# A new order for the opening of a Fourier mixing and ELU kernel: x by two queues, weights converted in three steps

## The chip, the core and the metric

The kernel runs on one core of a Trainium2 chip. The metric is the device time of one launch in microseconds (us). The kernel before took 2698.89 us, the median of three runs (2695.69 to 2701.08).

A core has five engines that run side by side and each keep the order of their own instructions: PE (TensorE, matrix products), DVE (VectorE), ACT (ScalarE), POOL (GpSimd) and SP (SyncE, which here only issues transfers). Transfers (DMA) are issued by SP and ACT on one kind of queue and by POOL on another. Engines wait for each other where data or a buffer needs it.

## The reference, cut to what matters

```python
# x (8, 3008, 256), filt_r and filt_i (1505, 256), all float32
X = np.fft.rfft(x, axis=1)
y = np.fft.irfft(X * (filt_r + 1j * filt_i)[None], n=3008, axis=1).astype(np.float32)

h = y.reshape(24064, 256) @ w_in             # w_in (256, 2048)
g = np.where(h > 0, h, np.exp(np.minimum(h, 0.0)) - 1.0)
out = (g @ w_out).astype(np.float32)         # w_out (2048, 256)
```

Both weights arrive as float64, and the kernel computes in float32. It fetches each number as a pair of 32-bit words and builds the float32 from the bits: this is the "conversion" that the text is about.

## The kernel before: what the change touches

The transform of length 3008 is done as 47 x 64 with small matrix products, and goes through memory (DRAM) twice: z holds the sums over 64, yd holds the first half of the way back. For a batch b the units are:

- `x_load`, `x_unit` (DVE: sum and difference), `a_unit` (PE psa, ACT copies), `z_write`: six chunks c.
- `z_read`, `b_unit` (PE psr, psi; DVE four products with the filter f; POOL subtracts and adds), `bi_unit` (PE pva, pvb; ACT copies), `y_write`: eight groups g.
- `y_read`, `n_unit` (PE psn, ACT copies, DVE four sums): six row blocks m.
- Then per block four "quads" q, a quarter of the 2048 columns each: `up_steps` (seven products with w_in[q], PE phs, pha, phd, with copies and ELU on ACT and DVE) and, a quad later, `down_steps` (seven products with w_out[q], PE po).

The first batch's transform stands alone in the opening; those of the other seven lie between quads. In the opening the filters are read into one large buffer ff, whose padding must be zero. In the quads w_in[q] is first needed in quad q, and w_out[q] in quad q + 1.

The 16 pieces of weights (512 KB each) are numbered k; q = k // 4, pieces 0 and 1 of four belong to w_in[q], 2 and 3 to w_out[q]. After the second of each pair four sums (s1, s2, s4, a21) prepare the seven-product scheme. One piece, before:

```python
def w_convert(k):
    wd = wds.pop(k)
    lo, hi = wd[:, :, 0], wd[:, :, 1]
    m, e = (kp.tile([P, 512], U32, tag=t, name=n) for t, n in (("k0", "wm"), ("k1", "we")))
    fl = kp.tile([P, 2, 512], FP32, tag="c", name="wfl")          # kp has one buffer of each
    f, l = fl[:, 0], fl[:, 1]
    nc.vector.tensor_scalar(out=m, in0=hi, scalar1=0x000FFFFF, scalar2=None, op0=ALU.bitwise_and)   # L509
    nc.scalar.activation(out=l, in_=lo, func=AXT.Identity, scale=2.0 ** -52)                        # L510
    nc.scalar.activation(out=f, in_=m, func=AXT.Identity, scale=2.0 ** -20, bias=1.0)               # L511
    nc.vector.tensor_scalar(out=e, in0=hi, scalar1=20, scalar2=0x7FF,
                            op0=ALU.logical_shift_right, op1=ALU.bitwise_and)                       # L513
    nc.vector.tensor_scalar(out=e, in0=e, scalar1=1151.0, scalar2=896.0, op0=ALU.min, op1=ALU.max)  # L515
    nc.vector.tensor_scalar(out=e, in0=e, scalar1=896.0, scalar2=8388608.0,
                            op0=ALU.subtract, op1=ALU.mult)                                         # L516
    nc.vector.scalar_tensor_tensor(out=e, in0=hi, scalar=0x80000000, in1=e,
                                   op0=ALU.bitwise_and, op1=ALU.bitwise_or)                         # L518
    nc.vector.tensor_tensor(out=f, in0=f, in1=l, op=ALU.add)                                        # L520
    # ... dst = f * e, one or two instructions (L528, L531)
    if j % 2 == 1:
        # ... the four sums (L535 to L538)
```

The opening, before:

```python
CONVERTS = {1: 6, 3: 7, 5: 8, 7: 9, 8: 10, 9: 11}
for k in range(2):
    w_fetch(k)                                  # POOL's queue
for c in range(NXC):                            # x: SP's queue, its table: ACT's
    x_load(0, c, nc.scalar, more[c - XBUFS] if c >= XBUFS else None)
nc.gpsimd.memset(ff, 0.0)
# ... gb, gr, gi
wait_x(3)                                       # POOL waits for the fourth chunk of x
w_fetch(2)
w_fetch(3)
wait_x(5)
for a in range(2):
    f_read_first(ff, a)                         # POOL's queue, 24 transfers
for c in range(NXC):
    x_unit(0, c); a_unit(0, c); z_write(0, c)
    if c in (0, 2):
        w_convert(c // 2)
for k in range(4, 7):
    w_fetch(k)
for k in range(2, 6):
    w_convert(k)
    w_fetch(k + 5)
z_read(0, 0); z_read(0, 1)
for g in range(NG + 2):
    if g >= 2: bi_unit(0, g - 2)
    if g < NG:
        b_unit(0, g, ff[:, g])
        if g + 2 < NG: z_read(0, g + 2)
    if g >= 2: y_write(0, g - 2)
    if g in CONVERTS: w_convert(CONVERTS[g])
    # ... w_fetch 11 and 12, x_load(1, 0) and (1, 1)
y_read(0, 0)
w_convert(12)
# ... POOL waits for y, then w_fetch 13, 14, 15
n_unit(0, 0)
# quads: w_convert 13 and 14 at the end of quad 0, 15 at the end of quad 1
```

Of the kernel before, what the change touches and what calls it, by code (L numbers as in the profile page):

```python
# [10 lines left out]
FP32 = mybir.dt.float32  # L11
# [10 lines left out]
N = 3008  # L22
# [78 lines left out]
def kernel(  # L101
# [38 lines left out]
    w_in, w_out = ([glob.tile([P, 7, 2, P], FP32, name="%s%d" % (n, i)) for i in range(4)] for n in ("wi", "wo"))  # L140

    fbufs = [glob.tile([P, 2, 2, D], FP32, name="f%d" % i) for i in range(FBUFS)]
    junk = glob.tile([P, 1], FP32, name="junk")
    fd = fdp.tile([NG, 2, 48, 2, 2, D], FP32, name="fd")

    xs, tas, tns, t1s, t2s, ss, t3s, t4s, zs, yds, ys, g_of, po_of, cs_, sds = ({} for _ in range(15))
# [1 line left out]
    def raw(src, row, ap, col=0):  # L148
        return bass.AP(tensor=src.tensor, offset=src.offset + row * D + col, ap=ap)
# [8 lines left out]

    def x_load(b, c, queue=nc.sync, place=None):

        t, w = place or (xp.tile([P, 2, 2, D], FP32, tag="xc", name="xc"), tap.tile([P, 2, P], FP32, tag="ta", name="ta"))
        xs[b, c], tas[b, c] = t, w
        queue.dma_start(w, ta_d[:, 2 * c:2 * c + 2, :])
        for h in range(2):
            i = XC * c + 2 * h
            r = slice(64 * h, 64 * h + 32)
            nc.sync.dma_start(t[r].rearrange("p k u d -> p k (u d)"),
                              raw(x, b * N + i, [[N1 * D, 32], [32 * N1 * D, 2], [1, 2 * D]]))  # L170
            r = slice(64 * h + 32, 64 * h + 64)
            for u in range(2):
                if i + u == 0:
                    nc.gpsimd.memset(t[r, :, 0, :], 0.0)
                else:
                    nc.sync.dma_start(t[r, :, u, :],  # L176
                                      raw(x, b * N + N1 - i - u, [[N1 * D, 32], [32 * N1 * D, 2], [1, D]]))

    def x_unit(b, c):
        t = xs[b, c]  # L180
# [299 lines left out]
    def w_fetch(k):  # L480
        q, j = divmod(k, 4)

        wd = wds[k] = wbufs[k % 5 if k < 12 else (2, 0, 1, 2)[k - 12]].bitcast(U32).rearrange("p c u d -> p (c u d)").rearrange("p (a w) -> p a w", w=2)
        if j < 2:
            srcs = [moe_w_in.bitcast(U32)[ts(j, P), ts(q, 1024)]]
        else:
            srcs = [moe_w_out.bitcast(U32)[ts(4 * q + 2 * (j - 2) + i, P), :] for i in range(2)]
        for i, s in enumerate(srcs):
            n = 512 // len(srcs)
            nc.gpsimd.dma_start(wd[:, ts(i, n), :].rearrange("p a w -> p (a w)"), s)  # L490

    def w_convert(k):

        q, j = divmod(k, 4)
        if j < 2:
            dst = w_in[q][:, 2 * j:2 * j + 2, :, :].rearrange("p j a c -> p a j c")
            shape = dict(a=2, j=2)
        else:  # L500
            dst = w_out[q][:, 0:4, j - 2, :]
            shape = None
        wd = wds.pop(k)
        lo, hi = wd[:, :, 0], wd[:, :, 1]
        m, e = (kp.tile([P, 512], U32, tag=t, name=n) for t, n in (("k0", "wm"), ("k1", "we")))
        fl = kp.tile([P, 2, 512], FP32, tag="c", name="wfl")
        f, l = fl[:, 0], fl[:, 1]

        nc.vector.tensor_scalar(out=m, in0=hi, scalar1=0x000FFFFF, scalar2=None, op0=ALU.bitwise_and)  # L509
        nc.scalar.activation(out=l, in_=lo, func=AXT.Identity, scale=2.0 ** -52)  # L510
        nc.scalar.activation(out=f, in_=m, func=AXT.Identity, scale=2.0 ** -20, bias=1.0)  # L511

        nc.vector.tensor_scalar(out=e, in0=hi, scalar1=20, scalar2=0x7FF,  # L513
                                op0=ALU.logical_shift_right, op1=ALU.bitwise_and)
        nc.vector.tensor_scalar(out=e, in0=e, scalar1=1151.0, scalar2=896.0, op0=ALU.min, op1=ALU.max)  # L515
        nc.vector.tensor_scalar(out=e, in0=e, scalar1=896.0, scalar2=8388608.0,  # L516
                                op0=ALU.subtract, op1=ALU.mult)
        nc.vector.scalar_tensor_tensor(out=e, in0=hi, scalar=0x80000000, in1=e,  # L518
                                       op0=ALU.bitwise_and, op1=ALU.bitwise_or)
        nc.vector.tensor_tensor(out=f, in0=f, in1=l, op=ALU.add)  # L520
        if shape:
            f, e = (t.rearrange("p (a j c) -> p a j c", **shape) for t in (f, e.bitcast(FP32)))
        else:

            f, e = (t.rearrange("p (i a e s) -> p i e a s", i=2, a=4, e=2) for t in (f, e.bitcast(FP32)))
            dst = dst.rearrange("p (i e) (a s) -> p i e a s", i=2, a=4)
        if shape:
            nc.vector.tensor_tensor(out=dst, in0=f, in1=e, op=ALU.mult)  # L528
        else:
            for i in range(2):  # L530
                nc.vector.tensor_tensor(out=dst[:, i], in0=f[:, i], in1=e[:, i], op=ALU.mult)  # L531
        if j % 2 == 1:
            w = (w_in if j < 2 else w_out)[q]
            a11, a21, a12, a22, s1, s2, s4 = (w[:, i] for i in range(7))
            nc.vector.tensor_tensor(out=s1, in0=a21, in1=a22, op=ALU.add)  # L535
            nc.vector.tensor_tensor(out=s2, in0=s1, in1=a11, op=ALU.subtract)
            nc.vector.tensor_tensor(out=s4, in0=a12, in1=s2, op=ALU.subtract)
            nc.vector.tensor_tensor(out=a21, in0=a11, in1=a21, op=ALU.subtract)  # L538

    def f_arrange():  # L540

# [16 lines left out]
    with tc.manual_schedule():  # L558


        CONVERTS = {1: 6, 3: 7, 5: 8, 7: 9, 8: 10, 9: 11}
        with tc.tile_pool(name="boot", bufs=1) as bp:
            ff = bp.tile([P, NG, 2, 2, D], FP32, name="ff")
            wbufs += [bp.tile([P, 2, 2, D], FP32, name="wb%d" % i) for i in range(2)]
            more = [(bp.tile([P, 2, 2, D], FP32, name="xb%d" % i), bp.tile([P, 2, P], FP32, name="tb%d" % i))
                    for i in range(NXC - XBUFS)]

            def wait_x(c):

                nc.gpsimd.tensor_copy(out=junk[0:1], in_=xs[0, c][0:1, 0, 0, 0:1])  # L570

            for k in range(2):
                w_fetch(k)
            for c in range(NXC):
                x_load(0, c, nc.scalar, more[c - XBUFS] if c >= XBUFS else None)
            nc.gpsimd.memset(ff, 0.0)
            for t, d in ((gb, gb_d), (gr, gr_d), (gi, gi_d)):
                nc.gpsimd.dma_start(t, d)
            wait_x(3)
            w_fetch(2)  # L580
            w_fetch(3)
            wait_x(5)
            for a in range(2):
                f_read_first(ff, a)
            for c in range(NXC):
                x_unit(0, c)
                a_unit(0, c)
                z_write(0, c)
                if c in (0, 2):
                    w_convert(c // 2)  # L590
            for k in range(4, 7):
                w_fetch(k)
            for k in range(2, 6):
                w_convert(k)
                w_fetch(k + 5)
            z_read(0, 0)
            z_read(0, 1)
            for g in range(NG + 2):
                if g >= 2:
                    bi_unit(0, g - 2)  # L600
                if g < NG:
                    b_unit(0, g, ff[:, g])
                    if g + 2 < NG:
                        z_read(0, g + 2)
                if g >= 2:
                    y_write(0, g - 2)
                if g in CONVERTS:
                    w_convert(CONVERTS[g])
                if g == 1:
                    w_fetch(11)  # L610
                if g == 4:
                    w_fetch(12)
                if g in (5, 6):
                    x_load(1, g - 5)
        yp = pool("yp", 2)
        gp = pool("gp", 2)
        ep = pool("ep", 2)
        op = pool("op", 1)
        y_read(0, 0)
        w_convert(12)  # L620
        nc.gpsimd.tensor_copy(out=junk[0:1], in_=t4s[0, 0][0:1, 0, 0:1])
        for k in (13, 14, 15):
            w_fetch(k)
        n_unit(0, 0)

# [3 lines left out]
        def at(quad, place, fn, *a):  # L631
            plan.setdefault((quad, place), []).append((fn, a))

        for c in range(2, XBUFS):
            at(c - 2, 0, x_load, 1, c)
        for k in (13, 14, 15):
            at(max(k - 14, 0), 1, w_convert, k)
        at(3, 1, f_arrange)
        for f in fbufs:
            at(4, 1, nc.vector.memset, f, 0.0)  # L640
        for b in range(B):
            t = (b - 1) * PER
            if b > 0:
                for c, s in enumerate((0, 2, 3, 4, 6, 7)):
                    at(t + s - 1, 0, x_unit, b, c)
                    at(t + s, 0, a_unit, b, c)
                    nb, nxt = (b, c + XBUFS) if c + XBUFS < NXC else (b + 1, c + XBUFS - NXC)
                    if nb < B:
                        at(t + s, 0, x_load, nb, nxt)
                    at(t + s, 0, z_write, b, c)  # L650
# [72 lines left out]
```

## Time and profile before

All from one profiled launch, whose span was 2697.7 us.

| engine | busy us | share of the span |
|---|---|---|
| PE | 2593.4 | 96% |
| DVE | 1870.0 | 69% |
| ACT | 1474.7 | 55% |
| POOL | 279.9 | 10% |

PE is the bound on average. But the page also cuts the span into 40 slices of 67 us and gives the busy share of each in tenths: PE has 1 and 6 in the first two and 9 in nearly all others. The opening is thus a stage of its own and is to be read by itself: in the timeline (instructions in order of time, with the idle time ahead of each and who ended it), in the chain of waits (followed back from the last instruction) and in busy times by stretch. "PEclk" is the clock that PE was granted, as a share of full speed; "DMA" the mean busy share of the 16 transfer engines. Some events of the opening:

| event | us from the start |
|---|---|
| first chunk of x in use (DVE) | 12.48 |
| POOL sees the last chunk of x | 29.06 |
| first z transfer issued | 28.45 |
| first transfer of the filters issued | 29.63 |
| first product with the filter (DVE) | 72.36 |
| last group's products begin | 114.50 |
| first matmul psn | 133.91 |
| PE without gaps from about | 174.60 |

In a line such as `90.02 1.11 DVE L509 TENSOR_SCALAR wm<-f 128x512 ...` the first number is the start, the second the duration, L509 the line of the kernel, and `wm<-f` says that tile wm is written from f.

### The profile page before, as it was taken

How to read it: one execution, taken by the hardware profiler on the slowest of the kernel's cores; microseconds unless marked ns; L12 is line 12 of the kernel's file. 1: busy time of each engine (PE TensorE's matmuls, PEld its weight loads, DVE VectorE, ACT ScalarE, POOL GpSimd, SP SyncE). 2: the span in 40 equal slices, each digit the busy share in tenths (PEclk: the TensorE clock that was granted, in tenths of full speed). 3: DMA queues.
4: the chain of work that ended last, by engine and by line, in shares of the span. 5: the costliest groups of instructions: out<-in, count | busy, mean ns of one | idle time of the engine just before them, and what ended most of it. 6: DMA issues, size and time to landing. Idle time of an engine off the chain costs nothing.

```text
span 2697.7 us, 37154 instructions
## 1 busy us (share of the span) xinstructions
PE 2593.4 (96%) x13376; PEld 2196.4 (81%) x13376; DVE 1870.0 (69%) x3243; ACT 1474.7 (55%) x2561; POOL 279.9 (10%) x325
## 2 busy tenths in 40 slices
PE   1689999999999999999999999999999999999998
PEld 1278888987889878988889887898789888899887
DVE  4876776667667677767766677676767767666665
ACT  2255555555556555555555555565556555555554
POOL 4311210002100120001200021000210012000000
PEclk7589999999999999999999999999999999999999
DMA  9545331434213431153314332143421233110010
GB/s 232 156 121 132 79 78 40 101 77 104 62 38 89 103 96 38 45 124 79 85 37 91 90 90 70 38 101 83 114 58 38 60 87 92 38 40 19 21 27 16
DMA packets 234934, 208.23 MB, mean 77 GB/s; under 512 B 134052, under 2 KB 201142, under 8 KB 234752
## 3 DMA queue, kind: packets, MB, share of 16 engines
q1 hardware_dynamic: 216096, 168.15, 25.3%
q0 software_dynamic: 17792, 36.93, 5.6%
q8 instruction: 106, 1.74, 0.3%
q10 hardware_dynamic: 864, 0.79, 0.1%
q14 instruction: 76, 0.62, 0.1%
HBM read 130.68 MB, written 78.12 MB: 77 GB/s over the span
## 4 chain that ended last, share of the span: by engine, by line
PE 94%; DMA 2%; DVE 2%; issue 1%; SPq 0%; ACT 0%; POOL 0%; ACTq 0%; DVEq 0%; POOLq 0%
PE po L426 42%; PE phs L344 25%; PE phd L344 12%; PE pha L344 6%; PE psn L296 3%; PE pva L239 2%; PE psr L239 2%; PE psa L194 2%; DMA z<-t 0%; DMA ff<-in_filt_i_dram 0%; DMA ta<-ta_t 0%; PE pvb L239 0%; SPq L176 0%; DMA t<-z 0%; DMA xb<-in_x_dram 0%
## 5 line engine op out<-in xcount | busy, mean ns | idle before, releaser
L426 PE MATMUL po<-g,wo 128*128 128x256 f32 (+1 forms) x5376 | 1298.1, 376 | 0.0
L426 PEld LDWEIGHTS po<-g,wo 128*128 128x128 f32 x5376 | 1016.3, 190 | 129.4 <-issue 15.4
L355 ACT ACTIVATE g<-phs 128x512 f32<-128x512 f32 (+1 forms) x576 | 339.0, 589 | 845.3 <-PE phs L344 844.6
L352 DVE TENSOR_TENSOR g<-phd,g 128x512 f32<-128x512 f32 (+1 forms) x384 | 259.6, 676 | 462.8 <-ACT e L362 277.8
L362 ACT ACTIVATE e<-e 128x512 f32<-128x512 f32 (+1 forms) x768 | 477.3, 622 | 24.4
L344 PE MATMUL phs<-ys,wi 128*128 128x256 f32 (+1 forms) x1536 | 388.9, 376 | 11.2 <-ACT g L355 11.2
L344 PE MATMUL phs<-y,wi 128*128 128x256 f32 (+1 forms) x1536 | 395.5, 380 | 0.0
L366 DVE SCALAR_TENSOR_TENSOR g<-e,g 128x512 f32<-128x512 f32 (+1 forms) x576 | 387.2, 672 | 0.0
L361 ACT ACTIVATE e<-g 128x512 f32<-128x512 f32 (+1 forms) x576 | 352.8, 613 | 36.7 <-DVE g L352 30.6
L344 PEld LDWEIGHTS phs<-y,wi 128*128 128x128 f32 x1536 | 285.1, 190 | 82.9 <-ACT t L267 34.1
L344 PEld LDWEIGHTS phs<-ys,wi 128*128 128x128 f32 x1536 | 292.4, 191 | 45.4 <-ACT g L355 12.3
L366 DVE SCALAR_TENSOR_TENSOR g<-e,phs 128x512 f32<-128x512 f32 (+1 forms) x192 | 130.0, 677 | 139.6 <-ACT e L362 139.6
L256 POOL TENSOR_TENSOR sr<-sr,sp 128x512 f32<-128x512 f32 x64 | 81.2, 1269 | 1265.3 <-DVE sp L253 1265.3
L344 PE MATMUL phd<-ys,wi 128*128 128x256 f32 (+1 forms) x768 | 193.9, 375 | 1.8 <-DVE g L352 1.8
L344 PE MATMUL pha<-y,wi 128*128 128x256 f32 (+1 forms) x768 | 194.0, 375 | 0.0
L344 PE MATMUL phd<-y,wi 128*128 128x256 f32 (+1 forms) x768 | 193.9, 375 | 0.0
L361 ACT ACTIVATE e<-phs 128x512 f32<-128x512 f32 (+1 forms) x192 | 113.0, 588 | 140.5 <-PE phs L344 139.6
L344 PEld LDWEIGHTS phd<-ys,wi 128*128 128x128 f32 x768 | 145.7, 190 | 19.0 <-DVE g L352 2.6
L344 PEld LDWEIGHTS pha<-y,wi 128*128 128x128 f32 x768 | 146.3, 191 | 16.6
L344 PEld LDWEIGHTS phd<-y,wi 128*128 128x128 f32 x768 | 145.7, 190 | 17.2 <-issue 0.4
L406 DVE TENSOR_TENSOR g<-g,g 128x512 f32<-128x512 f32 (+1 forms) x192 | 130.7, 681 | 6.7
L403 DVE TENSOR_TENSOR g<-g,g 128x512 f32<-128x512 f32 (+1 forms) x192 | 130.7, 681 | 6.6
(111 smaller groups left out, 2377.6 us busy)
## 6 DMA issues: line engine op xcount, KB each, us to landing
z<-t SPq DMA_DIRECT2D x96, 256.0 KB
t<-z SPq DMA_DIRECT2D x256, 96.0 KB
yd<-t SPq DMA_DIRECT2D x128, 192.0 KB
t<-yd SPq DMA_DIRECT2D x192, 128.0 KB
f<-fd POOLq DMA_DIRECT2D x112, 192.0 KB, 3.7
out_dram<-o SPq DMA_DIRECT2D x640, 32.0 KB
tn<-tn_t SPq DMA_DIRECT2D x48, 256.0 KB
xc<-in_x_dram SPq DMA_DIRECT2D x92, 128.0 KB
```

The costliest lines, as they stand in the source:

```text
L239: nc.tensor.matmul(ps[:, u:u + w, :], table[k, v, :], rhs[k, u:u + w, :], start=True, stop=True)
L256: nc.gpsimd.tensor_tensor(out=sr, in0=sr, in1=p, op=ALU.subtract)
L296: nc.tensor.matmul(ps[:, ts(q, P)], t[:, i - 4 * m, ds(dh * P, P)], w[:, i - 4 * m, :], start=True, stop=True)
L344: nc.tensor.matmul(ps[:, a, 0:h], w_in[q][:, COMBO[n], a, :], y[n], start=start and a == 0, stop=True, skip_group_check=True)
L352: nc.vector.tensor_tensor(out=g[o], in0=i0, in1=i1, op=ALU.add)
L355: nc.scalar.activation(out=g[o], in_=i0, func=AXT.Copy)
L361: nc.scalar.activation(out=e, in_=src, func=AXT.Relu, scale=-1.0)
L362: nc.scalar.activation(out=e, in_=e, func=AXT.Exp, scale=-1.0)
L366: nc.vector.scalar_tensor_tensor(out=g[n], in0=es[n], scalar=1.0, in1=src, op0=ALU.subtract, op1=ALU.max)
L403: nc.vector.tensor_tensor(out=b12, in0=b22, in1=b12, op=ALU.subtract)
L406: nc.vector.tensor_tensor(out=g["t4"], in0=g["b21"], in1=g["t2"], op=ALU.subtract)
L426: nc.tensor.matmul(po[i][:, u, 0:h], w_out[q][:, COMBO[n], a, :], g[n][:, a, :], start=q == 0 and a == 0 and n in (1, 3, 6, 4), stop=True, ...
```

## The change

Four things are changed, all in the opening and the first quads.

1. x of the first batch comes by two queues: the forward rows stay with SP, the mirrored rows go to POOL's queue, with the weights 0 and 1 between them. The table for all six chunks is one transfer on ACT's queue instead of six. POOL no longer waits for x; the filters follow in its queue.
2. The clearing of ff goes from POOL to ACT.
3. A conversion is three steps that can stand apart: `w_split` (two masks, DVE), `w_float` (four instructions, ACT) and `w_join` (sign, sum, product and, for every second piece, the four sums; DVE). The exponent is no longer shifted, clamped and scaled by three DVE instructions: it is masked in place, and two Relu instructions on ACT clamp it. The intent is less work for DVE and no waiting of one engine inside a conversion. Odd pieces below 8 use other buffers than even ones, so that two can be under way.
4. Pieces 10 to 15 are converted in quads 0 to 2 (before: 10 to 12 ahead of the first n_unit), 6 to 9 at other places, and the loads of the second batch's x begin later.

The core of the diff:

```diff
+    def w_split(k):
+        if k < 8 and k % 2:
+            a, c = (t4p.tile([P, 4, D], FP32, tag="t4", name=n)... for n in ("wme", "wfl"))
+            m, e, f, l = a[:, 0].bitcast(U32), a[:, 1].bitcast(U32), c[:, 0], c[:, 1]
+        else:
+            # ... kp tiles, as before
+        nc.vector.tensor_scalar(out=m, in0=hi, scalar1=0x000FFFFF, scalar2=None, op0=ALU.bitwise_and)
+        nc.vector.tensor_scalar(out=e, in0=hi, scalar1=0x7FF00000, scalar2=None, op0=ALU.bitwise_and)
+
+    def w_float(k):
+        nc.scalar.activation(out=l, in_=wds[k][:, :, 0], func=AXT.Identity, scale=2.0 ** -52)
+        nc.scalar.activation(out=f, in_=m, func=AXT.Identity, scale=2.0 ** -20, bias=1.0)
+        nc.scalar.activation(out=ef, in_=e, func=AXT.Relu, scale=-8.0, bias=edges[:, 0:1])
+        nc.scalar.activation(out=e, in_=ef, func=AXT.Relu, scale=-1.0, bias=edges[:, 1:2])
+
+    def w_join(k):
+        # ... or of the sign, f + l, product, four sums for odd k: as before
+        nxt = k + 5 if k < 8 else k + 3 if k > 9 else 16
+        if nxt < 16:
+            w_fetch(nxt)

-            for k in range(2):
-                w_fetch(k)
-            for c in range(NXC):
-                x_load(0, c, nc.scalar, more[c - XBUFS] if c >= XBUFS else None)
-            nc.gpsimd.memset(ff, 0.0)
+            nc.scalar.dma_start(tb, ta_d)
+            nc.scalar.memzero(ff)
+            for c in range(NXC):
+                if c < 2:
+                    w_fetch(c)
+                place = xb[c - XBUFS] if c >= XBUFS else xp.tile(...)
+                x_load(0, c, (place, tb[:, 2 * c:2 * c + 2]), nc.gpsimd)   # mirrored rows by POOL
             for t, d in ((gb, gb_d), (gr, gr_d), (gi, gi_d)):
                 nc.gpsimd.dma_start(t, d)
-            wait_x(3)
-            w_fetch(2)
-            w_fetch(3)
-            wait_x(5)
+            for k in (2, 3):
+                w_fetch(k)
             for a in range(2):
                 f_read_first(ff, a)
+            w_fetch(4)
 ...
+            w_split(0); w_float(0); chunk(0)           # chunk: x_unit, a_unit, z_write
+            w_split(1); w_float(1); w_join(0)
+            chunk(1); chunk(2); w_join(1)
+            for c in range(3, NXC):
+                chunk(c)
+            for g in range(2):
+                z_read(0, g)
+            w_split(2); w_float(2)
+            for k in range(3, 6):
+                w_split(k); w_float(k); w_join(k - 1)
+            w_join(5)
             for g in range(NG + 2):
+                k = {2: 6, 5: 7, 8: 8}.get(g)
+                if k: w_split(k)
                 # ... bi_unit, b_unit, z_read
+                if k: w_float(k)
                 # ... y_write
+                if k: w_join(k)
+            w_split(9); w_float(9); w_join(9)
         y_read(0, 0)
-        w_convert(12)
+        x_load(1, 0)
         n_unit(0, 0)
+        w_split(10); w_float(10)

-        for k in (13, 14, 15):
-            at(max(k - 14, 0), 1, w_convert, k)
+        for k in range(10, 16):                         # quad (k - 10) // 2; place 0 middle, 1 end
+            at((k - 10) // 2, k % 2, w_join, k)
+            if k < 15:
+                at((k - 10) // 2, k % 2, w_split, k + 1)
+                at((k - 10) // 2, k % 2, w_float, k + 1)
```

## The prediction

> **What bounds the kernel now.** I read the page's slices first, to see where TensorE is not busy.
>
> ```profile
> PE   1689999999999999999999999999999999999998
> PEclk7589999999999999999999999999999999999999
> ```
>
> Only the first two of the 40 slices (67 us each) fall short, so the change can win or lose only there. Next I cut the opening at the events that the chain of waits names, and asked for the busy times in those stretches (columns: stretch, its length, busy time of PE, weight loads, DVE, ACT, POOL, then the granted clock, the DMA share and GB/s).
>
> ```profile
> 29.06:61.16 32.10, 5.79 (x48) 4.12 (x48) 13.30 (x28) 5.51 (x10) 16.98 (x30) 0.61 1.03 236
> 61.16:72.36 11.20, 4.00 (x14) 1.76 (x14) 8.73 (x18) 3.08 (x5) 1.61 (x3) 0.50 0.93 276
> 72.36:133.91 61.55, 38.22 (x125) 10.81 (x123) 53.79 (x92) 15.71 (x29) 24.28 (x23) 0.50 0.53 149
> 133.91:174.60 40.69, 29.43 (x144) 26.56 (x144) 30.39 (x61) 19.39 (x36) 1.75 (x4) 0.80 0.42 109
> 220.00:400.00 180.00, 179.68 (x937) 147.19 (x938) 130.91 (x222) 99.13 (x170) 29.82 (x35) 1.00 0.37 90
> ```
>
> The reader sees three different limits: to 61 us the transfers (share about 1), from 72 to 134 us DVE (54 of 61.55 us), from 134 to 175 us none of them (waits between ACT, DVE and PE), and from then on PE. So I sum three stages: A up to the first product with the filter (72.36), B from there to the first matmul psn (61.55 long), C from psn until PE is saturated (40.7 long, to 174.6). The chain of waits gives what ends A and B:
>
> ```profile
> 33.13 11.07 DMA ff<-in_filt_i_dram
> ...
> 47.36 13.09 DMA z<-t
> 61.16 6.42 DMA t<-z
> 67.71 1.94 PE psr L239 x4
> ...
> 126.11 2.63 DMA yd<-t
> ```
>
> A ends with z written, read back and four matmul groups at half clock. The timeline of DVE shows one conversion inside B, and the timeline of ACT what the conversions do to others:
>
> ```profile
> 90.02 1.11 DVE L509 TENSOR_SCALAR wm<-f 128x512 uint32<-128x512 uint32 x1
> 91.05 1.49 DVE L513 TENSOR_SCALAR we<-f 128x512 uint32<-128x512 uint32 x1
> 92.57 0.43 DVE L515 TENSOR_SCALAR we<-we 128x512 uint32<-128x512 uint32 x1
> ...
> 101.80 0.69 DVE L251 TENSOR_TENSOR sr<-psr,ff 128x512 f32<-128x512 f32 x1 [2.11 <-PE psi L239]
> ```
> ```profile
> 124.48 0.63 ACT L511 ACTIVATE wfl<-wm 128x512 f32<-128x512 uint32 x1 [1.34 <-DVE wm L509]
> 125.02 0.58 ACT L267 ACTIVATE t<-pva 128x512 f32<-128x512 f32 x1
> ...
> 156.94 0.63 ACT L511 ACTIVATE wfl<-wm 128x512 f32<-128x512 uint32 x1 [1.33 <-DVE wm L509]
> 157.47 0.53 ACT L355 ACTIVATE g<-phs 128x448 f32<-128x448 f32 x1
> ```
>
> Twice a copy that PE or a transfer waits for (t at 125.02, g at 157.47) stands in ACT's queue behind a conversion that waits for DVE.
>
> **What the Trainium skill says.** "SBUF — State Buffer", section "Who interferes with whom": a DVE tensor_scalar in its two-port mode and a GpSimd instruction exclude each other. The trace agrees: the two masks of a conversion take 1.11 and 1.49 us right after a product, when POOL subtracts, and 0.42 us elsewhere. "TensorE: Matmul & The Clock Gate", section "What's actually happening": an idle array is clocked at half. The clock was 0.50 from 61 to 134 us; I keep that. "ScalarE: Activation LUTs", section "What ACT_TABLE_LOAD costs": an instruction costs about 186 ns + 0.833 ns per element, which gives 0.61 us for 512 (trace: 0.59) and, an estimate, 7.0 us for the new clearing of ff with 8192 elements; POOL's took 6.92. "DMA: Bandwidth & Descriptors", section "Queues, rings and completion order": the engines go round between the queues that have work. The trace fits: from 29 to 61 us z (3.1 MB), ff (3.0 MB) and weights share 236 GB/s, and both z and ff end near 60.
>
> **Stage A.** Removed: the memset of ff from POOL (6.92 us), POOL's two waits for x (the second ended at 29.06, and the filters were issued only then). Moved: half of x onto POOL's queue, between weights 0 and 1. The built program lets each kind of queue have eight transfers in flight, so POOL's seventh piece of x waits for weights 0 (9.1 us to landing before). POOL has 23 pieces of x (64 KB) at 0.55 us of issue, 12.7 us, behind two weights; with the waits for weights 0 and 1 I put the last x at 20 us issued and 24 landed. Check by bytes: x 3.08 + weights 1.05 + table 0.79 = 4.9 MB at 230 GB/s is 21 us from 2.5. Then g, weights 2 and 3; the filters start at 25 instead of 29.6. Before, weights 4 were issued 23.8 us after the filters began (53.40) and landed at 61.3. With z gone earlier I take 23 us: issued at 48, landed at 55.
>
> z is no longer the last: its first chunk can leave at 16 us (before 28.45, because SP's queue was full of x), chunks follow as x comes, and 3.1 MB against the filters at half of 240 GB/s end at 42 to 46; read back by 52, matmuls by 56. DVE ends later. After weights 4 at 55 its order is split 4 (0.8), join 3 with its four sums (2.0 + 1.6), split 5 (0.8), wait for float 5 and join 4 (2.0), join 5 with sums (3.6): 10.5 us. First product at 65.5. **A: -6.9 us.**
>
> **Stage B.** Without a conversion the pitch of two groups is 4.59 us (97.21 to 101.80): 2.5 of products, 2.1 waiting for PE, which needs the banks that the products free. Before, conversions 6, 7 and 8 stood whole in DVE's queue, and the pitches with one were 7.90, 9.60 and 8.11; from first to eighth product 42.1 us. Now only 6 and 7 lie between products. A split (1.1 + 1.5 beside POOL) goes where DVE waited for PE: 5.0 instead of 4.59. A join (0.61 + 0.72 + 0.7 = 2.0) likewise fits the next wait; with sums 3.6, so 6.1. The two subtractions and the clamp (2 x 0.46) leave DVE; four ACT instructions (2.3 us) lie beside the products. In all 2.8 + 5.4 (third group is bound by PE here) + 4.6 + 4.6 + 4.6 + 5.0 + 6.1 = 33.1. To the tail: products of group 7 2.5, split 8 2.5, ACT's float 8 2.3 and the two copies 1.1, then 7.9 us for y out and in, as before (126.0 to 133.91): 16.3. B is 49.4 instead of 61.55. **B: -12.1 us.**
>
> **Stage C.** This is the bill. Before, conversions 9 to 12 ran on DVE from 117 to 136.8, most of it while everybody waited for y. Now only 8 and 9 do; 10 to 15 are in stage C, where before only 13 to 15 were. DVE: 6 x 2.8 + 3 x 1.6 = 21.6 us for 3 x 3.85 + 2 x 1.6 = 14.8. ACT: 6 x 2.3 = 13.8 for 3 x 1.2. And each float stands on ACT ahead of copies that PE needs. Step by step from psn:
> - Float 10 follows the two copies of psn and waits for split 10 behind the four sums of y (psn + 5.4): done at 7.6, so the first copy g is at 7.6 instead of 5.3: +2.3.
> - Float 11 comes ahead of the exponentials of quad 0: +0.9 more at its tail (psn + 20.4 on DVE). Join 11 with sums and split 12 take 4.4, float 12 ends at 26.2; the copy that opened quad 1 at 157.47 (psn + 23.6) comes at 26.2: +2.6 in all.
> - Quad 1: float 13 delays the exponentials by 1.6, the moved pair of copies of the second batch by 1.0. DVE's tail is at 43.5; join 13 with sums, split 14, float 14 and the copies of psn follow in line, so quad 2 opens at psn + 50.9 instead of 40.7: +10.2.
> - Quad 2: join 14, split 15, join 15 put 7 us onto a DVE that is 73% busy when PE is the bound (130.91 of 180); its idle takes most: +1.
> **C: +11.2 us.**
>
> Sum: -6.9 - 12.1 + 11.2 = -7.8 us, from 2698.89 to 2691.1. The weight pieces are the same 16, and PE's work after that is unchanged, so nothing more comes later.
>
> **Rivals.** (1) The late conversions eat all of it: if the floats meet DVE worse in quads 1 to 3 (say 5 us per quad), C costs 18 to 20, and the time is 2699, no change. For it speaks that before, one such meeting cost 9.4 us of PE (the wait of PE for g at 157.47); against it that joins are now a step later than their floats, so ACT waits only for masks. (2) C costs only the added DVE time less its idle, about 4 us, since PE runs ahead with products of the quad before: 2684. For it: quads 0 and 1 have idle DVE (30.4 of 40.7 busy). Against: DVE and ACT keep their order, idle time before a late operand can't be used. (3) Bytes hold A: by 61 us 13 MB had moved at 216 GB/s, and after needs about the same before its first product; if POOL's 64 KB pieces leave gaps or the filters crawl behind z, weights 4 land at 60 and A gains 2: 2696. (4) z was really what mattered and weights 4 come with 52: A gains 10 and the time is 2688.
>
> **Range and chances.** A may be off by 4 us, B by 3, C by 6, the measurement by 3 (2695.69 to 2701.08): together about 8, so 8 in 10 within 2680 to 2701. 2% is 54 us, more than all idle of PE that the three stages could give back without new bounds; slower by 54 would need a new stall every quad. Faster 0.02, within 2% 0.97, slower 0.01.
>
> **What would show it.** A: filters issued from about 25 us, z landed by 46, first product at 65 and ended by DVE's joins. B: pitches of 4.6 to 6.1 instead of 7.9 to 9.6, no copy t held for more than a float. C: psn at 115; ACT's copies g at the starts of quads 1 and 2 right behind floats 12 and 14; PE saturated at about 167 instead of 174.6. If first product and psn come as said but the total doesn't fall, the weight conversions in C are dearer than I take them; if psn comes after 125, A is held by bytes.

## The result and the profile after

| | before | after |
|---|---|---|
| median of four runs each, us | 2699.17 (2695.69 to 2701.08) | 2706.28 (2704.31 to 2711.18) |
| profiled span, us | 2697.7 | 2704.8 |

The ratio of after to before is 1.0031, with a 95% interval of 1.0013 to 1.0048: the change costs about 7 us, 0.3% and clear of the noise, where the prediction had a gain of 7.8. It lies outside the predicted range (2680 to 2701).

The slices of the page of after:

```profile
PE   3679999999999999999999999999999999999998
PEclk7689999999999999999999999999999999999999
```

PE does more in the first slice (3 tenths for 1) and less in the third (7 for 8). Everything from the fourth slice on looks as before, so the loss is again in the opening. The busy times of after in the stretches that answer to those of before (columns: stretch, its length, PE, weight loads, DVE, ACT, POOL, granted clock, DMA share, GB/s):

```profile
25.31:48.90 23.59, 4.27 (x44) 3.23 (x37) 5.82 (x12) 8.08 (x14) 12.35 (x22) 0.58 1.06 241
48.90:73.81 24.91, 7.83 (x20) 2.12 (x20) 10.33 (x23) 5.17 (x8) 6.00 (x11) 0.50 0.98 211
73.81:125.66 51.85, 33.59 (x117) 10.72 (x117) 42.01 (x63) 18.66 (x32) 23.54 (x20) 0.60 0.51 147
125.66:177.81 52.15, 31.97 (x145) 28.50 (x145) 31.86 (x65) 27.60 (x49) 2.88 (x5) 0.73 0.43 109
177.81:205.62 27.81, 26.80 (x145) 23.88 (x146) 21.30 (x42) 16.18 (x30) 8.74 (x8) 0.92 0.51 120
205.62:2704.80 2499.18, 2484.95 (x12857) 2126.92 (x12855) 1732.58 (x2989) 1410.28 (x2445) 213.14 (x243) 1.00 0.28 70
```

The filters now start at 25.31, z is written at 48.90 (SP's first read back), the first product is at 73.81, psn at 125.66; quad 2 opens at 177.81 and quad 4 (the first of the next block) at 205.62. Stage B lost 12 us of DVE work and became 9.7 us shorter; the stage from psn to quad 2 has 8.2 us more of ACT (27.60 for 19.39), 1.5 more of DVE, 2.5 more of PE, and became 11.46 longer. The last line shows that nothing later matters. Before, from quad 2 to quad 4 and from there to the end:

```profile
174.60:198.77 24.17, 24.16 (x145) 22.09 (x146) 18.86 (x37) 13.99 (x26) 7.62 (x8) 1.00 0.58 138
198.77:2697.70 2498.93, 2484.95 (x12857) 2126.94 (x12855) 1732.56 (x2988) 1410.31 (x2445) 214.77 (x243) 1.00 0.29 70
```

The rest took 2498.93 us with the same 2484.95 of PE.

| stage | before, us | after, us | difference | predicted |
|---|---|---|---|---|
| A: start to first product | 72.36 | 73.81 | +1.45 | -6.9 |
| B: to psn | 61.55 | 51.85 | -9.70 | -12.1 |
| C: to quad 2 | 40.69 | 52.15 | +11.46 | +10.2 |
| C: quad 2 to quad 4 | 24.17 | 27.81 | +3.64 | +1 |
| the rest | 2498.93 | 2499.18 | +0.25 | 0 |

The differences add up to the 7.1 us between the spans. The chain of waits of after, in its opening (start, length, what):

```profile
25.31 10.55 DMA ff<-in_filt_r_dram
...
39.30 9.88 DMA ff<-in_filt_r_dram
50.02 13.13 DMA wb<-in_moe_w_in_dram
...
73.81 0.69 DVE sr L255
...
117.97 2.61 DMA yd<-t
```

Before, this chain went over z written and read back; now z is off it, and the 13.13 us that weights 4 take to land are on it. The timeline of DVE shows what that costs, and a second thing, inside stage B:

```profile
63.17 0.43 DVE L511 TENSOR_SCALAR wm<-wb 128x512 uint32<-128x512 uint32 x1 [23.91 <-DMA wb<-in_moe_w_in_dram]
...
84.49 1.38 DVE L528 SCALAR_TENSOR_TENSOR we<-f,we 128x512 uint32<-128x512 uint32 x1
85.80 1.75 DVE L530 TENSOR_TENSOR wfl<-wfl 128x512 f32<-128x512 f32 x1
...
117.24 0.68 DVE L530 TENSOR_TENSOR wfl<-wfl 128x512 f32<-128x512 f32 x1
```

DVE stands idle for 23.91 us until weights 4 land, at 63.17 for the 55 that I had. In the join of piece 6, right behind a product, sign and sum take 1.38 and 1.75 us; in the join of piece 8, with no POOL work beside it, such a sum takes 0.68. Stage C, in the timelines of ACT and then PE (the bracket is the idle time just before, and who ended it):

```profile
152.81 0.72 ACT L522 ACTIVATE we<-we,edges 128x512 uint32<-128x512 f32 x1
153.44 0.52 ACT L359 ACTIVATE g<-phs 128x448 f32<-128x448 f32 x1
...
174.36 0.63 ACT L518 ACTIVATE wfl<-wm 128x512 f32<-128x512 uint32 x1 [1.38 <-DVE wm L511]
174.89 0.70 ACT L521 ACTIVATE we<-we,edges 128x512 f32<-128x512 uint32 x1
175.63 0.72 ACT L522 ACTIVATE we<-we,edges 128x512 uint32<-128x512 f32 x1
...
177.21 0.54 ACT L359 ACTIVATE g<-phs 128x448 f32<-128x448 f32 x1
```
```profile
154.01 1.86 PE L348 MATMUL phs<-ys,wi 128*128 128x224 f32 x4 [9.82 <-ACT g L359]
...
169.23 0.92 PE L430 MATMUL po<-g,wo 128*128 128x224 f32 x4
177.81 1.86 PE L348 MATMUL phs<-ys,wi 128*128 128x224 f32 x4 [7.66 <-ACT g L359]
```

The same two openings, of quads 1 and 2, in the timeline of PE before:

```profile
158.05 1.86 PE L344 MATMUL phs<-ys,wi 128*128 128x224 f32 x4 [9.37 <-ACT g L355]
...
174.60 1.02 PE L344 MATMUL phs<-ys,wi 128*128 128x224 f32 x4 [1.23 <-ACT g L355]
```

In after the copy g that opens quad 1 or 2 stands in ACT's queue behind a whole float (at quad 2 with two copies of psn between), as the prediction had it. At quad 1 PE waits much as before (9.82 us for 9.37); at quad 2 it waits 7.66 us, where before it waited 1.23. And when it restarts there, four matmuls take 1.86 us, twice the 0.92 of just before the wait.

### The profile page after: what moved, and what is told of

Read it like the earlier page. It is cut to its first block, busy times and chain, and to the rows that moved or that the text cites. A ratio compares the mean times of both kernels' runs of the same rounds, so it can differ in the third digit from the quotient of the medians.

```text
span 2704.8 us, 37139 instructions
## 1 busy us (share of the span) xinstructions
PE 2598.0 (96%) x13376; PEld 2200.1 (81%) x13376; DVE 1856.7 (69%) x3213; ACT 1502.5 (56%) x2594; POOL 284.7 (11%) x344
## 4 chain that ended last, share of the span: by engine, by line
PE 93%; DMA 2%; DVE 2%; ACT 1%; issue 1%; POOL 1%; SPq 0%; DVEq 0%; POOLq 0%
PE po L430 42%; PE phs L348 24%; PE phd L348 12%; PE pha L348 6%; PE psn L300 3%; PE pva L243 2%; PE psr L243 2%; PE psa L198 1%; DMA ff<-in_filt_r_dram 1%; DMA wb<-in_moe_w_in_dram 0%; DMA f<-in_moe_w_in_dram 0%; PE pvb L243 0%; DMA xc<-in_x_dram 0%; PE psi L243 0%; DVE g L370 0%
```

## The experiments

Theory T had three parts. TA: the first product is late because weights 4 stand behind the 24 filter transfers in POOL's queue. TB: the joins in stage B lengthen because DVE's instructions with two SBUF inputs wait for POOL's subtractions. TC: C is longer because ACT's four instructions per piece stand ahead of the copies g. The rivals: the bytes hold A whatever the order; C's length comes from the conversions' DVE work; the new order of x itself costs. e1 to e5 were each timed in 12 runs and e6 in 8, against the kernel before on the same chip (median 2698.78 us beside e1 to e4, 2697.92 beside e5 and e6); e7 to e10 are one run each. Stages are read from one profiled run, and the runs of one kernel spread over some 5 us (e5: 2689.72 to 2694.91), so a stage that differs by 1 or 2 us is not by itself a difference between kernels.

**e1: weights 4 to 6 fetched ahead of the filters.**

```diff
-            for a in range(2):
-                f_read_first(ff, a)
             w_fetch(4)
 ...
             w_join(1)
+            for a in range(2):
+                f_read_first(ff, a)
```

> The changed kernel with weights 4, 5 and 6 ahead of the filters in POOL's queue; nothing else. Theory (the place of weights 4 behind the filters sets stage A, because DVE then stands idle from 39 to 63 us): weights 4 land near 33 us, DVE has joined piece 5 by 50, the filters land some 7 us later than the 57 of the changed kernel, first product at 64 to 66 instead of 73.8, the whole 6 to 8 us under the changed kernel (2698 to 2700). Rival (bytes set stage A, the order only says who comes last): first product at 70 to 73, the whole 0 to 3 us under the changed kernel.

Measured: 2700.27 us, ratio to before 1.0005 (0.9996 to 1.0013), so 6 us less than after. The DVE timeline of e1, and PE's:

```profile
36.70 0.42 DVE L511 TENSOR_SCALAR wm<-wb 128x512 uint32<-128x512 uint32 x1
...
66.44 0.69 DVE L255 TENSOR_TENSOR sr<-psr,ff 128x512 f32<-128x512 f32 x1 [18.98 <-PE psi L243]
```
```profile
61.98 1.94 PE L243 MATMUL psr<-t,gb 48*64 48x256 f32 x4 [31.44 <-DMA t<-z]
```

Piece 4 is split at 36.70 instead of 63.17. DVE is then done early and waits for PE, and PE for z read back: the first product is at 66.44, 7.4 us earlier than in after and near the 65.5 of the prediction, but by way of z. TA holds, and the rival of bytes (70 to 73) falls: the same bytes in another order allow an earlier first product. Part of the gain is lost again: in the stage table below, B is 2 us longer than in after.

**e2: the clamp back on DVE**, three instructions there in place of one, and two fewer on ACT, for each piece.

```diff
-        nc.vector.tensor_scalar(out=e, in0=hi, scalar1=0x7FF00000, ... bitwise_and)
+        # shift and mask, min and max, subtract and mult on DVE, as before
 ...
-        nc.scalar.activation(out=ef, in_=e, func=AXT.Relu, scale=-8.0, bias=edges[:, 0:1])
-        nc.scalar.activation(out=e, in_=ef, func=AXT.Relu, scale=-1.0, bias=edges[:, 1:2])
```

> The changed kernel with the exponent's clamp back on DVE (split has four DVE instructions, float two on ACT). Theory (in stage C the floats stand on ACT ahead of copies that PE waits for, and their length sets the loss): quad 2 opens 46 to 48 us after psn instead of 52.2, stage B 2 us longer, the whole 3 to 5 us under the changed kernel (2701 to 2703). Rival (the work of DVE sets stage C): quad 2 opens 52 or more after psn, the whole 2 to 5 us over the changed kernel.

Measured: 2700.03 us, ratio to before 1.0006 (0.9997 to 1.0015), 6.3 us less than after. From psn to quad 2 it takes 45.39 us for 52.15. PE's line at quad 2 in e2:

```profile
171.68 1.86 PE L348 MATMUL phs<-ys,wi 128*128 128x224 f32 x4 [4.93 <-ACT g L359]
```

Up to quad 2 DVE has more work than in after (35.89 us for 31.86), ACT less (21.03 for 27.60), and the stage is 6.8 us shorter, a little more than the theory expected: how long the floats stand ahead of the copies on ACT sets this part. TC holds, and the rival (52 or more) falls. But 4.7 of the 11.46 us remain with the clamp on DVE. Presumably they go with the three late pieces more that the quads hold than before, on DVE and ACT; no run here divides them further.

**e3: pieces 10 to 15 converted whole where they were before.**

```diff
+            for k in range(10, 13):
+                w_convert(k); w_fetch(k + 3)          # ahead of the first n_unit
-        w_split(10); w_float(10)
-        # ... joins, splits and floats of 10 to 15 in quads 0 to 2
+        for k in (13, 14, 15):
+            at(max(k - 14, 0), 1, w_convert, k)
```

> The changed kernel with the late pieces as before: 10 to 12 whole and ahead of the first n_unit, 13 and 14 at the end of quad 0, 15 at the end of quad 1. Theory (the earlier psn can't be used, since DVE's conversions are only moved from a wait into the quads): psn at 125.7 as in the changed kernel, but its sums wait for DVE until about 137; quad 2 opens at about 175, the whole like before (2697 to 2701). Rival (the place in the quads is what costs, and the gain at psn is real): quad 2 opens near 168, the whole 2690 to 2693.

Measured: 2698.37 us, ratio 1.0000 (0.9992 to 1.0009). psn comes at 123.52, 10 us earlier than before, but DVE is at conversions until 135.42 and makes the sums of y only then. In the timeline of DVE in e3:

```profile
134.81 0.69 DVE L590 TENSOR_TENSOR wi<-wfl,we 128x512 f32<-128x512 f32 x1
135.42 0.38 DVE L323 TENSOR_TENSOR ys<-y 128x224 f32<-128x224 f32 x1
```

From psn to quad 2 it takes 48.02 us, and from there all is as before (24.17). In this profile quad 2 opens at 171.54, between the theory (175) and the rival (168) and 3 us earlier than before; in the medians of the runs none of that shows (2698.37 and 2698.78). So of the 10 us at psn most is not used when the pieces are only moved: ahead of the sums they hold these, behind them they hold the copies.

**e4: only the opening's new order (parts 1 and 2 of the change) in the kernel before.**

> The kernel before with only the opening's new order (x by two queues, one table, the clearing of ff on ACT, no waits of POOL for x); conversions and their places as before. Theory (weights 4 behind the filters set stage A, not x): z lands some 12 us earlier, weights 4 land at 60 to 63, first product at 70 to 73 as before (72.4), the whole within 2 us of before. Rival (x by two queues does gain what it was meant to): first product at 66, the whole 5 to 7 us under before.

Measured: 2697.22 us, ratio 0.9995 (0.9986 to 1.0004). The first product comes 2.9 us earlier (69.47; 70 to 73 was expected), psn 0.5 (133.40). Most of what is lost, 1.7 us, goes between the first and the second group's products (4.47 us apart for 2.77 before): DVE waits 2.00 us for PE there, and PE for z read back. From the second group to the last the pitches are those of before. The order of x costs nothing, so that rival falls; by itself it brings nothing that these runs can tell from zero.

**e5: the edits of e1 and e2 together.**

> The changed kernel with both edits: weights 4 to 6 ahead of the filters, and the clamp on DVE. Theory (they mend two different stages, A and C, so their gains of 6.0 and 6.3 us add): first product at 66 to 67, psn at 120 to 121, quad 2 opens 45 to 46 us after it, the whole 2692 to 2695. Rival (one limit behind both, so that the second gain is taken back by a later wait): 2698 to 2700.

Measured: 2691.90 us, ratio to before 0.9977 (0.9969 to 0.9986), 14.4 less than after. The two gains of about 6 add (the 2 us more than their sum are within the noise of the three medians), so they are two causes. Taking weights 4 to 6 first has a price: the filters come last, in this profile DVE waits 1.44 us for one of them at 68.89, and psn comes at 122.81, where 120 to 121 was expected.

**e6: the version built from these.** Weights 4 to 6 first; one piece more ahead of the groups and in them, so that only 11 to 15 are left for the quads; the clamp on ACT up to piece 9, where ACT has room, and on DVE from 10 on.

```diff
-            for k in range(3, 6):
+            for k in range(3, 7):
 ...
-                k = {2: 6, 5: 7, 8: 8}.get(g)
+                k = {2: 7, 5: 8, 8: 9}.get(g)
-            w_split(9); w_float(9); w_join(9)
+            w_split(10); w_float(10); w_join(10)
-        for k in range(10, 16):
+        for k in range(11, 16):
         # ... the filters moved as in e1, the clamp chosen by piece
```

> Weights 4 to 6 ahead of the filters; piece 6 converted ahead of the groups, in DVE's idle time before the first product; pieces 7 to 9 in the groups, 10 ahead of n_unit, 11 to 15 in the quads; the clamp on DVE from piece 10 on, on ACT before. Theory (what counts is how much conversion lies in DVE's early idle time and how short the floats in the quads are): first product at 66 to 67, psn at 120 to 121, quad 2 opens 41 to 44 us after it, the whole 2686 to 2691. Rival (the late pieces cost nothing more once the floats are short): as the run with both edits, 2692 to 2695.

Measured in 8 runs: 2690.77 us, ratio to before 0.9972 (0.9962 to 0.9982). It beats both kernels, but is not clearly apart from e5: psn is 3.1 us earlier, yet the step from psn to quad 2 takes 44.14 (expected 41 to 44). With the numbers shifted by one the joins with four sums came to the middle of the quads; that this is the reason is likely, but no run takes it apart. In its timeline of ACT:

```profile
135.35 0.58 ACT L365 ACTIVATE e<-g 128x448 f32<-128x448 f32 x1 [2.25 <-DVE g L370]
```

Here ACT waits for DVE, which had join 11 with its sums and split 12 from 127.20 to 132.6, ahead of what ACT needs.

**e7: after, without POOL's work in groups 2 and 5.** It leaves out POOL's subtraction and addition in these two groups of the first batch, so its output lacks them; one run.

```diff
+        if b > 0 or g not in (2, 5):
             nc.gpsimd.tensor_tensor(out=sr, in0=sr, in1=p, op=ALU.subtract)
             nc.gpsimd.tensor_tensor(out=si, in0=si, in1=q, op=ALU.add)
```

> The changed kernel, but POOL's subtraction and addition are left out in groups 2 and 5 of the first batch, whose products the joins of pieces 6 and 7 follow (so part of the first batch is computed without those terms; its time is what is looked at). Theory (a join beside POOL waits for it: that is the term of 2.0 us that came out as 3.9): the sign and the sum of the joins take 0.69 us each instead of 1.38 and 1.75, the two pitches with a join 4.6 and 6.2 instead of 6.17 and 7.87 us. Rival (the joins wait for their floats or for PE): the pitches stay.

The timeline of DVE in e7, at the join of piece 6:

```profile
85.19 0.68 DVE L529 SCALAR_TENSOR_TENSOR we<-f,we 128x512 uint32<-128x512 uint32 x1
85.79 0.68 DVE L531 TENSOR_TENSOR wfl<-wfl 128x512 f32<-128x512 f32 x1
```

Sign and sum take 0.68 each, for 1.38 and 1.75. The pitch of the groups falls from 6.17 to 4.40 us and from 7.87 to 6.10, and B from 51.85 to 46.77, more than the 3.5 us of the two pitches. TB holds.

The stages of the seven, from their profiles, in us:

| | first product | B | psn to quad 2 | quad 2 to 4 | median |
|---|---|---|---|---|---|
| e1 | 66.44 | 53.84 | 52.03 | 27.41 | 2700.27 |
| e2 | 73.86 | 52.43 | 45.39 | 26.47 | 2700.03 |
| e3 | 72.79 | 50.73 | 48.02 | 24.17 | 2698.37 |
| e4 | 69.47 | 63.93 | 40.37 | 24.16 | 2697.22 |
| e5 | 66.76 | 56.05 | 44.76 | 26.16 | 2691.90 |
| e6 | 66.05 | 53.62 | 44.14 | 26.63 | 2690.77 |
| e7 | 74.51 | 46.77 | 50.85 | 27.52 | 2700.6 (one run) |

**e8 to e10: why weights 4 took 13 us to land.** One run each; only the landing of weights 4 is read. e8 puts a one-word write by DVE, behind the masks of piece 4, into the tile that z is read into, so that the read back begins later. e9 lets POOL read a word of those masks before it fetches pieces 5 to 8; by this edit the sign of piece 3 is read from a buffer that piece 8 has already taken. e10 leaves out eight of the 24 filter transfers, and its output lacks that part of the filter.

```diff
+        if late:                                   # e8, in z_read for group 0
+            nc.vector.memset(t[0:1, 0, 0:1], 0.0)
+                if k == 4:                         # e9, behind w_split(4)
+                    nc.gpsimd.tensor_copy(out=junk[0:1], in_=wts[4][0].bitcast(FP32)[0:1, 0:1])
+                    for n in range(5, 9): w_fetch(n)
-                for r0, n in ((24, 16), (40, 7)):  # e10
+                for r0, n in ((24, 16), (40, 7)) if a == 0 else ():
```

> The changed kernel, but z is read back for groups 0 and 1 only after the masks of piece 4. The place of weights 4 in the queue is settled; open is why they took 13.1 us from issue to landing (50.02 to 63.17) and not 7 to 8. Theory P (the eight small filter transfers still ahead in the same queue, which move only 120 to 150 GB/s with all engines busy): the landing stays at 62 to 63.5. Rival R (z read back from 48.9 takes half of the engines' turns): weights 4 land at 58 to 60. The first product comes later than 73.8 in both, at 75 to 78, because the read back now follows the landing.

> The changed kernel, but pieces 5 to 8 are fetched only after the masks of piece 4, so that nothing stands behind weights 4 in their queue. Theory P (small filter transfers ahead): weights 4 still land at 62 to 63.5. Rival N (2 MB of weights behind share the engines with weights 4): they land at 57 to 59. Rival R (z read back): no change by this edit, 62 to 63.5. The first product is later in all, at 78 to 82, because piece 5 comes late.

> The changed kernel without eight of the 24 filter transfers, the small ones of the mirrored rows of the second half of the filters (1 KB runs on 16 and 7 partitions); their part of the filter stays zero, so the output lacks it. Theory P: weights 4 are issued at about 42 to 45 and land within 7 to 9 us, and the first product comes at 62 to 65, limited by z read back. Rivals R and N: they are issued at 42 to 45 too, but still need 11 to 13 us to land.

| | weights 4 issued | landed | between | z read back from | engines' time for POOL's queue | for SP's queue (z) |
|---|---|---|---|---|---|---|
| after | 50.02 | 63.17 | 13.1 | 48.90 | 9.7 | 3.9 |
| e2 (same order) | 49.90 | 61.37 | 11.5 | 49.14 | 8.2 | 3.4 |
| e3 (same order) | 50.89 | 62.15 | 11.3 | 50.09 | 8.0 | 3.5 |
| e7 (same order) | 52.34 | 63.88 | 11.5 | 50.69 | 7.7 | 3.8 |
| e8 | 51.62 | 60.20 | 8.6 | 61.01 | 8.8 | 0.0 |
| e9 | 51.42 | 60.46 | 9.0 | 51.95 | 6.6 | 2.1 |
| e10 | 42.29 | 53.54 | 11.3 | 53.13 | 10.9 | 0.8 |
| e4 | 52.91 | 60.45 | 7.5 | 55.87 | 7.6 | 0.1 |
| before | 53.40 | 61.28 | 7.9 | 60.73 | 6.3 | 1.7 |

"Landed" is where DVE, which waits for it, starts on piece 4. The last two columns add up the durations of the trace's packets that start between issue and landing, by kind of queue, over the 16 engines.

The four profiles with the order of after spread from 11.3 to 13.1 us, so after's 13.1 is the top of it. Without the read back (e8) it is 8.6, without the weights behind (e9) 9.0; with a third of the filter transfers left out (e10) it is still 11.3, though the fetch goes out 8 us earlier and the first product comes at 64.17. So theory P, the small transfers alone, falls for the landing. Neither rival wins alone: e8 still has the weights behind and e9 still has the read back, and both landed later than the rival in question expected (58 to 60, 57 to 59).

The two columns of packets say how the rivals share. In the four profiles with after's order z read back takes 3.4 to 3.9 us of the engines. Where it hardly runs in that time, in e8 and also in e4, where it was issued only 3 us after weights 4, the landing takes 8.6 and 7.5 us. What stands behind in POOL's own queue is the smaller part: in e9 this queue needs 6.6 us, in the four 7.7 to 9.7. (In after these were weights 5 to 7, 1.5 MB; weights 8 went out only at 64.83.) In e10, with next to no read back, nearly all of the 11.3 us is POOL's own queue, whose fetches followed each other closely. So the read back explains some 3.5 us of the landing; that split rests on single runs with a spread of 2 us.

The first products missed what was expected in e8 and e9: 72.16 for 75 to 78, and 83.02 for 78 to 82. In e8 it came 1.65 us earlier than in after, although z was read back 12 us later.

## Why the prediction was wrong, step by step

**A, predicted 65.5, came 73.81: the step that failed is "issued at 48, landed at 55".** The order of x did as said: filters at 25.31 (predicted 25), ff cleared on ACT, z written at 48.90 (predicted 42 to 46, before 60.73), the first group on PE from 57.80. The fetch of weights 4 went out at 50.02, 2 us late, and took 13.1 us to landing where I had 7, a figure taken from the 7.9 of before. There weights 5 to 8 followed too, but of z only the last writes (1.7 us of the engines) ran beside it. I had used "z gone earlier" only as relief; its read back, which the change had just pulled into the same stretch, was the new neighbour and took 3.9 us of the engines. From 63.17 on the 10.5 us of DVE that I worked out took 10.64 (the terms that I gave add up to 10.8). Rival (3) named the right object, "weights 4 land at 60", but with 3 us too little and for the wrong reason: it was bytes that were to hold A, and e1 moves the same bytes and gains 7.4 us. The cause that matters is the queue place: e1 takes the whole wait for weights 4 away.

**B, predicted 49.4, came 51.85: the term mis-sized is the join of 2.0 us.** Beside POOL it takes 3.8 (1.38 + 1.75 + 0.7). The pitch with the join of piece 6 was 6.17 where I had 4.6, that with piece 7 7.87 where I had 6.1. Those are 3.3 us, slightly more than the miss. I had cited the exclusion for masks only. "SBUF — State Buffer", section "Who interferes with whom", also says that a DVE instruction with two SBUF inputs contends with a GpSimd instruction that reads SBUF; e7 agrees, with 0.68 and 0.68 once POOL is silent. The product instructions, which take one input from PSUM, stay at 0.68 in all of it.

**C, predicted +11.2, came +15.1: the mechanism was right, the term mis-sized is the "+1" for quad 2 and after.** Up to quad 2 the count gave 50.9 us after psn and the profile shows 52.15. The copies stand where they were put: 133.42 behind float 10 (predicted psn + 7.6, so 133.3), 153.44 behind float 12 (psn + 27.8, predicted 26.2). But I judged quad 2 by DVE's idle time alone. PE arrives there after 7.66 us of waiting and runs at half clock: from the restart to the start of the 13th matmul 4.6 us go by where before, with a wait of 1.23, 2.4 did. "TensorE: Matmul & The Clock Gate", section "What's actually happening", which the prediction used for stage B, would have told it here too; the stretch's clock is 0.92 for 1.00 before. That is about 2.3 of the 3.64 us; another 1.0 is PE idle in that stretch (27.81 less 26.80), most of it one wait of 0.80 for DVE behind join 15. So DVE's part was the +1 that I had, and the clock is what was missing. The 1.26 us by which C up to quad 2 exceeded the count are not traced; PE is busy 2.54 us longer there, at a clock of 0.73 for 0.80, so the clock may have a part in them too.

Rival (1), that the late conversions eat all, had the total nearest (2699), and C lies between its 18 to 20 and my 11.2. That it came nearest is luck: A, which it left as I had it, lost 8.35 us. The misses, 8.35 in A, 2.4 in B and 3.9 in C, all point one way. In A and B I let a moved operation keep the duration it had in its old surroundings, and in C I let PE keep its clock over a longer wait.

## What to carry to other kernels

Where a change moves work, list for each moved piece the neighbours that it will have on its queue, its engine and its memory port, and size it by a row of the profile that has those neighbours, not by its old row. In a queue that keeps its order, look for what the next stage needs first. Here the place counted for more than the bytes: three fetches of weights moved ahead of the 24 filter transfers were worth 6 us. Taking two short instructions per piece from ACT, which feeds PE, was worth another 6, although DVE had two more for them.

## What the runs showed that I had not expected

- Busy transfer engines can move very different amounts: in after their share was 1.06 at 135 GB/s from 45 to 55 us (the last of z written, then filter pieces, weights and the first read back), and 1.06 at 241 GB/s from 25.31 to 48.90. That small pieces are the reason is not shown: in the second stretch z's packets of 1 KB took 57 ns each, while in the first the packets of 4 KB on POOL's queue took 519 ns, for 308 in the second.
- The same two DVE instructions took 1.38 and 1.75 us beside POOL and 0.68 without it (e7).
- PE's first four matmuls after a wait took 1.86 us after 4.93 (e2), 7.66 and 9.82 us of waiting, and 1.02 before, after one of 1.23. The length of the last wait alone does not decide: in after such four took 1.86 us at 135.80, too, after a wait of only 0.63.
